# Hash attention and adapter routing: single transposes between score matmuls, value matmuls by key block, crossbar turns, a last pair by thirds

## The chip, the cores and the metric

The kernel runs on one core of a Trainium2 chip. The metric is the time of one execution on the device, in microseconds (us), lower is better. A profiled execution gives the trace: start and duration of every instruction on the matmul engine (PE; its weight loads are shown as PEld), on the vector (DVE), scalar (ACT) and GpSimd (POOL) engines, and what the queues (SP's, ACT's and POOL's) issue as DMAs.

## The reference

Two stages. The first is attention in which a query sees only the keys that have the same hash: six sign bits of a random projection.

```python
q_bits = (np.einsum('bhsd,dk->bhsk', q, proj) > 0)     # k_bits likewise
mask = q_bucket[:, :, :, None] == k_bucket[:, :, None, :]
scores = np.where(mask, scale * q @ k.T, -1e9)
attn = np.exp(scores - scores.max(-1)) / (sum + 1e-9)
x = attn @ v                                           # (4, 8, 768, 64)
```

The second takes x as 3072 tokens of 512 features. Each token is routed to the best two of eight adapters of rank 16 and gets their weighted outputs added.

```python
logits = x @ w_gate                       # 512 -> 8
w = softmax over the two largest logits
out = x + sum over the two e of w[e] * (x @ A[e]) @ B[e]
```

There are 4 batches, 8 heads, 768 positions and head size 64. All is float32 outside; the matmuls of scores, values and adapters run in bf16 with float32 sums.

## The kernel before, in words

**Tiling.** Two heads of a batch make a pair; there are 16 pairs, four to a batch, worked off in the loop of `run` (L340). A position sits at partition p, place t (six places), so 768 = 128 x 6. Each pair has 9 slots: a slot computes 1024 columns of scores (keys on partitions, queries along the row) into one of two PSUM tiles `s` (L178), and ACT takes their exp into `P` in SBUF (L193). Twelve key blocks of 768 columns fill the nine slots.

**The hash mask is part of the score matmul.** Operand `aug` holds 71 rows: 64 of q or k, 6 sign rows of plus or minus one half, and one constant row. The sign products take away so much where a bit differs that the exp vanishes. A uniform tiny weight (the matrix `eps`, L70) is added in the value sum, so that a query with no key in its bucket averages all values.

**What prepares a pair.** `load` (L107) issues q, k and v of a pair on SP's queue, two pairs ahead. `trans` (L135) turns q and k on PE, four 128x128 blocks at a time into a PSUM tile `t`, and DVE copies them to `qkT` (L147). `hash` (L149) multiplies by the projection in four 128x32 tiles of PE; DVE makes signs, and SP issues eight small DMAs that carry them to the sign rows of `aug` (L164). `cast` (L168) brings q and k to bf16 in `aug`, both halves on DVE (L172).

**What follows the scores.** `pvmm` (L196) sums P times V per query block: six key blocks and the uniform one, seven matmuls of 65 columns (64 values and the sum of weights). `norm` (L212) divides. `xtrans` (L231) turns x for the adapter matmuls on PE, `lgz` (L243) computes logits and the rank-16 products, `route` (L254) picks two adapters and weights the products, `zmtrans` (L284) turns these, and `delta` (L296) multiplies by B, adds x and stores.

**Order.** Every engine's order is the order of the calls, written out by hand in `run`. The adapter stage of a finished batch lies in two later pairs (`moe_slot`, L312): logits and routing in one, six deltas in the next. After the last pair the adapter stage of the last batch stands alone (L369 to L381).

```python
                if s == 0:
                    self.load(p + 2)
                    self.norm(p - 1, 0)
                    self.trans(p + 1, 1)
```

PSUM: two `s` tiles of two banks, two `t` tiles, one for value sums, one (`m`) for the adapter stage. [...]

Of the kernel before, what the change touches and what calls it, by code (L numbers as in the profile page):

```python
# [19 lines left out]
class Emitter:  # L20


    def __init__(self, ctx, tc, q, k, v, proj, w_gate, A, Bm, out):
# [11 lines left out]
        self.n_pairs = B * H // 2  # L35
# [6 lines left out]
        one = lambda n: ctx.enter_context(tc.tile_pool(name=n, bufs=1))  # L42
        self.singles = one("singles")
        self.natp = ctx.enter_context(tc.tile_pool(name="natp", bufs=3))
        self.qktp = ctx.enter_context(tc.tile_pool(name="qktp", bufs=2))
        self.sgp = ctx.enter_context(tc.tile_pool(name="sgp", bufs=2))
        self.pp = ctx.enter_context(tc.tile_pool(name="pp", bufs=2))
        self.xp = ctx.enter_context(tc.tile_pool(name="xp", bufs=2))
        self.smallp = ctx.enter_context(tc.tile_pool(name="smallp", bufs=4))
        ps = lambda n, b: ctx.enter_context(  # L50
            tc.tile_pool(name=n, bufs=b, space=bass.MemoryType.PSUM))
        self.ps_s = ps("ps_s", 2)
        self.ps_t = ps("ps_t", 2)
        self.ps_v = ps("ps_v", 1)
        self.ps_m = ps("ps_m", 1)


        sg = self.singles
        self.ident = sg.tile([P, P], F32, name="ident")
        make_identity(nc, self.ident)  # L60
        self.ident_bf = sg.tile([P, P], BF16, name="ident_bf")
        nc.vector.tensor_copy(out=self.ident_bf, in_=self.ident)

        self.proj2 = sg.tile([P, 32], F32, name="proj2")
        nc.vector.memset(self.proj2, 0.0)
        nc.sync.dma_start(out=self.proj2[0:64, 0:6], in_=proj)
        nc.sync.dma_start(out=self.proj2[64:128, 6:12], in_=proj)

        self.eps = sg.tile([P, P], BF16, name="eps")
        nc.vector.memset(self.eps, 2.0 ** -56)  # L70

        self.aug = []
        for i in range(2):
            a = sg.tile([P, 4, S], BF16, name=f"aug{i}")
            for h in range(2):
                nc.vector.memset(a[64:96, 2 * h, :], 1.0)
                nc.vector.memset(a[64:96, 2 * h + 1, :], -1.5)
            self.aug.append(a)

        self.vb = []  # L80
        for i in range(3):
            a = sg.tile([P, 2, T + 1, D + 1], BF16, name=f"vb{i}")
            nc.gpsimd.memset(a[:, :, 0:T, D:D + 1], 1.0)
            nc.gpsimd.memset(a[:, :, T:T + 1, D:D + 1], float(T))
            self.vb.append(a)
        nD = self.Dm // P
        self.nD = nD
        self.wa = sg.tile([P, nD, self.LZ], BF16, name="wa")
        self.Bcat = sg.tile([self.ER, self.Dm], BF16, name="Bcat")
        self.w_gate, self.A, self.Bm = w_gate, A, Bm  # L90

        self.nat, self.vn, self.qkT, self.sgn, self.P_, self.pv = {}, {}, {}, {}, {}, {}
        self.x, self.xb, self.xT, self.lz, self.tp = {}, {}, {}, {}, {}
        self.rt, self.zm, self.zmT, self.acc, self.sc = {}, {}, {}, {}, {}

    def load_moe(self):
        nc, P = self.nc, self.P
        nc.gpsimd.dma_start(out=self.wa[:, :, 0:self.E],
                            in_=self.w_gate.rearrange("(t p) e -> p t e", p=P))
        for t in range(self.nD):  # L100
            nc.gpsimd.dma_start(
                out=self.wa[:, t, self.E:].rearrange("p (e r) -> p e r", e=self.E),
                in_=self.A[:, t * P:(t + 1) * P, :].rearrange("e p r -> p e r"))
        nc.gpsimd.dma_start(out=self.Bcat, in_=self.Bm.rearrange("e r d -> (e r) d"))


    def load(self, p):  # L107
        if p >= self.n_pairs:
            return
        nc = self.nc  # L110
        b, h = p // self.PPB, 2 * (p % self.PPB)
        n = self.natp.tile([self.P, 2, 2, self.T * self.D], F32, tag="nat", name=f"nat{p}")
        for i, src in enumerate((self.q, self.k)):
            nc.sync.dma_start(out=n[:, i], in_=src[b, h:h + 2].rearrange(
                "h (p t) d -> p h (t d)", t=self.T))
        vn = self.natp.tile([self.P, 2, self.T, self.D], F32, tag="vn", name=f"vn{p}")
        nc.sync.dma_start(out=vn.rearrange("p h t d -> p h (t d)"), in_=self.v[b, h:h + 2].rearrange(
            "h (p t) d -> p h (t d)", t=self.T))
        self.nat[p], self.vn[p] = n, vn

    def vcast(self, p):
        if p >= self.n_pairs:
            return
# [9 lines left out]


    def trans(self, p, g):  # L135
        if p >= self.n_pairs:
            return
        nc, P, D = self.nc, self.P, self.D
        if g == 0:
            self.qkT[p] = self.qktp.tile([P, 2 * self.S], F32, tag="qkT", name=f"qkT{p}")  # L140
        ps = self.ps_t.tile([P, 512], F32, tag="t", name=f"tr{p}_{g}")
        for j in range(4):
            idx, u = divmod(4 * g + j, 3)
            nc.tensor.transpose(out=ps[:, j * P:(j + 1) * P],  # L144
                                in_=self.nat[p][:, idx % 2, idx // 2, u * P:(u + 1) * P],
                                identity=self.ident)
        nc.vector.tensor_copy(out=self.qkT[p][:, g * 512:(g + 1) * 512], in_=ps)  # L147

    def hash(self, p):  # L149
        if p >= self.n_pairs:  # L150
            return
        nc = self.nc
        ps = self.ps_t.tile([self.P, 384], F32, tag="t", name=f"hs{p}")
        for j in range(4):
            nc.tensor.matmul(out=ps[32 * j:32 * j + 32, :], lhsT=self.proj2,  # L155
                             rhs=self.qkT[p][:, j * 384:(j + 1) * 384], start=True, stop=True)
        sgn = self.sgp.tile([self.P, 384], BF16, tag="sgn", name=f"sgn{p}")
        nc.vector.tensor_scalar(out=sgn, in0=ps, scalar1=0.0, scalar2=0.5,  # L158
                                op0=ALU.is_gt, op1=ALU.subtract)
        aug = self.aug[p % 2]  # L160
        for j in range(4):
            av = aug[64:70, j, :].rearrange("p (u e c) -> p u e c", e=2, c=self.P)
            for e in range(2):
                nc.sync.dma_start(out=av[:, :, e, :],  # L164
                                  in_=sgn[32 * j + 6 * e:32 * j + 6 * e + 6, :].rearrange(
                                      "p (u c) -> p u c", c=self.P))

    def cast(self, p, e):  # L168
        if p >= self.n_pairs:
            return  # L170
        av = self.aug[p % 2][0:64].rearrange("p j (u e c) -> p (j u) e c", e=2, c=self.P)
        self.nc.vector.tensor_scalar(  # L172
            out=av[:, :, e, :],
            in0=self.qkT[p][64 * e:64 * e + 64, :].rearrange("p (j c) -> p j c", c=self.P),
            scalar1=2.0 ** -5, scalar2=None, op0=ALU.mult)


    def score(self, p, s):  # L178
        nc, S, P = self.nc, self.S, self.P
        if s == 0:  # L180
            self.P_[p] = self.pp.tile([P, 2 * self.T * S], BF16, tag="P", name=f"P{p}")
        aug = self.aug[p % 2]
        ps = self.ps_s.tile([P, 1024], F32, tag="s", name=f"s{p}_{s}")
        at, end = s * 1024, (s + 1) * 1024
        while at < end:
            kt, q0 = divmod(at, S)
            h, kt = divmod(kt, self.T)
            n = min(512 - at % 512, S - q0)
            o = at - s * 1024
            nc.tensor.matmul(out=ps[:, o:o + n], lhsT=aug[0:71, 2 * h + 1, kt * P:(kt + 1) * P],  # L190
                             rhs=aug[0:71, 2 * h, q0:q0 + n], start=True, stop=True)
            at += n
        nc.scalar.activation(out=self.P_[p][:, s * 1024:end], in_=ps, func=ACT.Exp, scale=128.0)  # L193


    def pvmm(self, p, h, i0, i1):  # L196
        if p < 0:
            return
        nc, S, T, D = self.nc, self.S, self.T, self.D
        vb = self.vb[p % 3]  # L200
        if i0 == 0:
            self.pv[p, h] = self.ps_v.tile([self.P, T, D + 1], F32, tag="v", name=f"pv{p}_{h}")
        pv = self.pv[p, h]
        base = h * T * S
        for i in range(i0, i1):
            for kt in range(T + 1):
                o = base + kt * S + i * self.P
                lhsT = self.P_[p][:, o:o + self.P] if kt < T else self.eps
                nc.tensor.matmul(out=pv[:, i, :], lhsT=lhsT, rhs=vb[:, h, kt, :],  # L209
# [220 lines left out]
```

The softmax here doesn't subtract the row's maximum and nothing guards it: scores larger than these inputs give would overflow.

## Time and profile before

| | |
|---|---|
| three timed executions | 214.92, 220.12, 220.92 us; median 220.12 |
| the profiled execution, first to last instruction | 216.4 us |
| busy: PE, DVE, ACT, POOL | 178.0, 142.9, 144.1, 63.4 us |
| score exps (L193) | 144, mean 1024 ns |
| value matmuls (L209), with P and with eps | 1152 and 192 |
| float32 transposes of q and k (L144) | 192 |
| hash matmul passes (L155) | 128 |
| q and k casts on DVE (L172) | 32, mean 998 ns |
| sign DMAs (L164) | 128 of 4.5 KB, 720 ns to issue (median) |
| loads of q, k, v | 48 of 384 KB |
| DMA traffic | 26.39 MB, mean 122 GB/s |

Busy time of an engine is the time in which at least one of its instructions ran. Matmuls are pipelined: one's duration is longer than the distance to the next. Idle time is put down to what ended it, the releaser.

### The profile page before, as it was taken

How to read it: one execution, taken by the hardware profiler on the slowest of the kernel's cores; microseconds unless marked ns; L12 is line 12 of the kernel's file. 1: busy time of each engine (PE TensorE's matmuls, PEld its weight loads, DVE VectorE, ACT ScalarE, POOL GpSimd, SP SyncE). 2: the span in 40 equal slices, each digit the busy share in tenths (PEclk: the TensorE clock that was granted, in tenths of full speed). 3: DMA queues.
4: the chain of work that ended last, by engine and by line, in shares of the span. 5: the costliest groups of instructions: out<-in, count | busy, mean ns of one | idle time of the engine just before them, and what ended most of it. 6: DMA issues, size and time to landing. Idle time of an engine off the chain costs nothing.

```text
span 216.4 us, 5569 instructions
## 1 busy us (share of the span) xinstructions
PE 178.0 (82%) x2288; PEld 123.5 (57%) x2288; DVE 142.9 (66%) x303; ACT 144.1 (67%) x153; POOL 63.4 (29%) x98
## 2 busy tenths in 40 slices
PE   1647999999999997998979987989999879774341
PEld 0314286865868674756656866657678656463200
DVE  7771528675686768698756689796766875634541
ACT  2003679998999987677969976868999858730000
POOL 1694420623416050604133503305144110101000
PEclk9995569999999999999999999999999999997555
DMA  5895406062442616180746042533815000420024
GB/s 144 293 25 82 169 11 217 9 224 71 160 156 76 224 22 209 9 309 11 253 168 215 15 152 76 191 132 141 283 46 186 3 9 3 197 100 0 0 118 173
DMA packets 22874, 26.39 MB, mean 122 GB/s; under 512 B 8897, under 2 KB 21313, under 8 KB 22849
## 3 DMA queue, kind: packets, MB, share of 16 engines
q1 hardware_dynamic: 18016, 25.77, 35.2%
q0 software_dynamic: 4832, 0.27, 3.9%
q8 instruction: 18, 0.29, 0.6%
q14 instruction: 8, 0.06, 0.1%
HBM read 19.42 MB, written 6.29 MB: 119 GB/s over the span
## 4 chain that ended last, share of the span: by engine, by line
PE 52%; DVE 22%; DMA 9%; SPq 8%; issue 5%; ACT 2%; POOLq 0%; POOL 0%; DVEq 0%
PE s L190 20%; PE pv L209 12%; SPq L164 7%; PE tr L144 7%; PE hs L155 5%; DVE acc L303 5%; DMA nat<-in_k_dram 5%; PE dl L301 3%; DMA aug<-sgn 3%; DVE aug L172 3%; DVE sgn L158 2%; PE xtp L238 2%; DVE zm L276 2%; DMA nat<-in_q_dram 2%; DVE x L225 2%
## 5 line engine op out<-in xcount | busy, mean ns | idle before, releaser
L193 ACT ACTIVATE P<-s 128x1024 bf16<-128x1024 f32 x144 | 141.6, 1024 | 47.1 <-PE s L190 43.6
L190 PE MATMUL s<-aug 71*128 71x512 bf16 (+1 forms) x384 | 89.9, 336 | 5.0 <-DMA aug<-sgn 4.8
L209 PEld LDWEIGHTS <-P 128*128 128x128 bf16 x1152 | 51.3, 98 | 14.8 <-DVE x L225 1.0
L209 PE MATMUL pv<-vb,P 128*128 128x65 bf16 x1152 | 53.8, 194 | 0.9 <-DVE x L225 0.9
L190 PEld LDWEIGHTS <-aug 71*128 71x128 bf16 x384 | 32.5, 100 | 28.8 <-issue 13.0
L229 POOL CAST xb<-x 128x768 bf16<-128x768 f32 x16 | 13.2, 825 | 115.3 <-DVE x L225 115.3
L147 DVE COPY qkT<-tr 128x512 f32<-128x512 f32 x48 | 33.0, 690 | 14.1 <-PE tr L144 12.5
L144 PE MATMUL tr<-ident,nat 128*128 128x128 f32 x192 | 32.9, 296 | 8.1 <-DMA nat<-in_q_dram 3.9
L209 PE MATMUL pv<-vb,eps 128*128 128x65 bf16 x192 | 37.4, 195 | 0.0
L144 PEld LDWEIGHTS tr<-ident,nat 128*128 128x128 f32 x192 | 25.2, 152 | 14.4 <-issue 5.6
L172 DVE TENSOR_SCALAR aug<-qkT 64x1536 bf16<-64x1536 f32 x32 | 31.9, 998 | 0.9
L223 DVE RECIPROCAL ri<-pv 128x6 f32<-128x6 f32 x32 | 6.2, 193 | 29.5 <-PE pv L209 29.4
L303 DVE SCALAR_TENSOR_TENSOR acc<-dl,rt,x 128x512 f32<-128x512 f32 x24 | 17.9, 745 | 6.0 <-PE dl L301 6.0
L209 PEld LDWEIGHTS <-eps 128*128 128x128 bf16 x192 | 18.9, 98 | 0.0
L225 DVE TENSOR_TENSOR x<-pv,ri 128x384 f32<-128x384 f32 x32 | 17.8, 557 | 1.2
L126 POOL CAST vb<-vn 128x768 bf16<-128x768 f32 x16 | 13.3, 833 | 13.7 <-DMA vn<-in_v_dram 13.7
L128 POOL TENSOR_TENSOR vs<-vn 128x384 f32<-128x384 f32 x16 | 16.7, 1044 | 0.0
L301 PE MATMUL dl<-Bcat,zmT 128*128 128x512 bf16 x24 | 10.3, 431 | 7.7 <-DVE acc L303 6.8
L155 PE MATMUL hs<-qkT,proj 128*32 128x384 f32 x128 | 15.8, 542 | 0.0
L158 DVE TENSOR_SCALAR sgn<-hs 128x384 bf16<-128x384 f32 x16 | 8.9, 558 | 8.6 <-PE hs L155 7.0
L250 PE MATMUL lz<-wa,xT 128*128 128x136 bf16 x96 | 7.7, 235 | 4.3 <-DVE zm L276 3.6
L238 PE MATMUL xtp<-ident_bf,xb 128*128 128x128 bf16 x96 | 8.0, 219 | 3.0 <-POOL xb L229 1.4
(35 smaller groups left out, 79.6 us busy)
## 6 DMA issues: line engine op xcount, KB each, us to landing
nat<-in_q_dram SPq DMA_DIRECT2D x16, 384.0 KB
nat<-in_k_dram SPq DMA_DIRECT2D x16, 384.0 KB
vn<-in_v_dram SPq DMA_DIRECT2D x16, 384.0 KB
out_dram<-acc SPq DMA_DIRECT2D x12, 512.0 KB
aug<-sgn SPq DMA_DIRECT2D x128, 4.5 KB
wa<-in_moe_A_dram POOLq DMA_DIRECT2D x4, 32.0 KB, 3.1
Bcat<-in_moe_B_dram POOLq DMA_DIRECT2D x1, 128.0 KB, 3.5
proj<-in_proj_dram SPq DMA_DIRECT2D x2, 1.5 KB
```

Of the source, the lines that this page charges most:

```text
L128: nc.gpsimd.tensor_add(out=s3, in0=vn[:, :, 0:3, :], in1=vn[:, :, 3:6, :])
L144: nc.tensor.transpose(out=ps[:, j * P:(j + 1) * P], in_=self.nat[p][:, idx % 2, idx // 2, u * P:(u + 1) * P], identity=self.ident)
L147: nc.vector.tensor_copy(out=self.qkT[p][:, g * 512:(g + 1) * 512], in_=ps)
L155: nc.tensor.matmul(out=ps[32 * j:32 * j + 32, :], lhsT=self.proj2, rhs=self.qkT[p][:, j * 384:(j + 1) * 384], start=True, stop=True)
L164: nc.sync.dma_start(out=av[:, :, e, :], in_=sgn[32 * j + 6 * e:32 * j + 6 * e + 6, :].rearrange("p (u c) -> p u c", c=self.P))
L172: self.nc.vector.tensor_scalar(out=av[:, :, e, :], in0=self.qkT[p][64 * e:64 * e + 64, :].rearrange("p (j c) -> p j c", c=self.P), scalar1 ...
L190: nc.tensor.matmul(out=ps[:, o:o + n], lhsT=aug[0:71, 2 * h + 1, kt * P:(kt + 1) * P], rhs=aug[0:71, 2 * h, q0:q0 + n], start=True, stop=True)
L193: nc.scalar.activation(out=self.P_[p][:, s * 1024:end], in_=ps, func=ACT.Exp, scale=128.0)
L209: nc.tensor.matmul(out=pv[:, i, :], lhsT=lhsT, rhs=vb[:, h, kt, :], start=(kt == 0), stop=(kt == T))
L225: nc.vector.tensor_tensor(out=self.x[b][:, :, c:c + D], in0=pv[:, :, 0:D], in1=ri.unsqueeze(2).to_broadcast([P, T, D]), op=ALU.mult)
L301: nc.tensor.matmul(out=ps, lhsT=self.zmT[b][:, i * P:(i + 1) * P], rhs=self.Bcat, start=True, stop=True)
L303: nc.vector.scalar_tensor_tensor(out=self.acc[b][:, i, :], in0=ps, scalar=self.rt[b][:, i:i + 1], in1=self.x[b][:, i, :], op0=ALU.mult, op ...
```

## The change

The class keeps its stages but nearly every function and the whole order are new.

- **Transposes and copies.** `T1` transposes one 128x128 block; `score` takes a list of such calls and puts one after each of its matmuls. Each of the four operands (q and k of two heads) has its own PSUM tile and a copy of 384 columns (`tcopy`). `aug` is laid out by halves (places 0 to 2, then 3 to 5), so that key block kt is place `tok(kt)`.
- **Cast.** One half on DVE, the other on POOL.
- **Hash.** The two partition halves are multiplied separately, in 64x32 tiles of PE, into two PSUM tiles; four sign DMAs of six rows of 1536 bytes instead of eight.
- **Values.** `uni` adds the uniform weight for all six query blocks in one matmul of 390 columns; `pvk` then runs by key block, all six query blocks for one key block, so a key block can start when its own exps are there.
- **Turn.** `turn` casts x to bf16 on POOL and issues a transposing DMA on SP's queue in place of six PE transposes and a DVE copy. The second last pair keeps PE's way (`to_bf`, `turn_pe`), the last has its own.
- **Order.** Loads are three pairs ahead and split over slots 5, 6 and 7; the adapter stage is spread over four pairs (`moe1`); the adapter's weights are loaded in pairs 2 and 3. PSUM is now two `s`, one `m`, one `n`, two `v`.
- **Start.** Loads by heads on two queues, twelve matmuls on zeros, and for pair 0 and half of pair 1 hash matmuls that write their result at the sign rows' partitions, so that DVE puts signs into `aug` itself.
- **Last pair.** Scores run by thirds of the queries (two places of six at a time); values, norm, turn, logits and routing follow each third.

```diff
-        for j in range(4):
-            idx, u = divmod(4 * g + j, 3)
-            nc.tensor.transpose(out=ps[:, j * P:(j + 1) * P],
-                                in_=self.nat[p][:, idx % 2, idx // 2, u * P:(u + 1) * P],
-                                identity=self.ident)
-        nc.vector.tensor_copy(out=self.qkT[p][:, g * 512:(g + 1) * 512], in_=ps)
+    def T1(self, p, j, u, n=False):
...
+        nc.tensor.transpose(out=self.tr[p, j][:, u * P:(u + 1) * P],
+                            in_=self.nat[p][:, j % 2, j // 2, u * P:(u + 1) * P],
+                            identity=self.ident)
+    def tcopy(self, p, j, eng=None):
...
+        f = self.nc.scalar.copy if eng == "act" else self.nc.vector.tensor_copy
+        f(out=self.qkT[p][:, j, :], in_=self.tr[p, j][:, 0:384])
+    def cast(self, p, e, js=slice(0, 4), eng=None, psum=False):
...
+            (nc.gpsimd if eng == "pool" else nc.vector).tensor_scalar(
+                out=out, in0=in_, scalar1=2.0 ** -5, scalar2=None, op0=ALU.mult)
+    def hash(self, p, js=(0, 1, 2, 3)):
...
+        for j in js:
+            for e in range(2):
+                nc.tensor.matmul(out=ps[e][32 * j:32 * j + 32, 0:384],
+                                 lhsT=self.proj3[64 * e:64 * e + 64, :],
+                                 rhs=self.qkT[p][64 * e:64 * e + 64, j, :], start=True, stop=True)
+    def sign(self, p, js=(0, 1, 2, 3)):
...
+        for e in range(2):
+            nc.vector.tensor_scalar(out=sgn[r, e, :], in0=ps[e][r, 0:384], scalar1=0.0, scalar2=0.5,
+                                    op0=ALU.is_gt, op1=ALU.subtract)
...
+        for j in js:
+            nc.sync.dma_start(out=aug[64:70, j, :],
+                              in_=sgn[32 * j:32 * j + 6, :, :].rearrange("b e c -> b (e c)"))
+    def score(self, p, s, between=()):
...
+            nc.tensor.matmul(out=out, lhsT=aug[0:71, 2 * h + 1, kt * P:(kt + 1) * P],
+                             rhs=rhs, start=True, stop=True)
+            at += w
+            if between:
+                f = between.pop(0)
+                if f:
+                    f()
+        nc.scalar.activation(out=self.P_[p][:, s * 1024:end], in_=ps, func=ACT.Exp, scale=128.0)
...
+    def uni(self, p, h):
...
+        self.nc.tensor.matmul(out=pv, lhsT=self.eps,
+                              rhs=self.vb[p % 3][:, h, T:T + 1, :].to_broadcast([self.P, T, D + 1]),
+                              start=True, stop=False, skip_group_check=True)
+    def pvk(self, p, h, *kts):
...
+        for kt in kts:
+            for i in range(T):
+                o = (h * T + kt) * S + i * P
+                self.nc.tensor.matmul(out=pv[:, i, :], lhsT=self.P_[p][:, o:o + P],
+                                      rhs=vb[:, h, self.tok(kt), :], start=False,
+                                      stop=(kt == T - 1), skip_group_check=True)
+    def turn(self, p):
...
+        nc.gpsimd.tensor_copy(out=xb, in_=self.x[b][:, :, hp * P:(hp + 1) * P])
+        nc.sync.dma_start_transpose(out=self.xT[b][:, hp, :, :], in_=xb.rearrange("p t f -> p (t f)"))
+    def start(self):
...
+        for i in range(12):
+            nc.tensor.matmul(out=w, lhsT=self.wz[:, 0:128], rhs=self.wz, start=True, stop=True)
...
+        for j in (0, 1):
+            for f in self.tb(0, j, j == 1):
+                f()
+        self.tcopy(0, 0)
+        self.hash_here(0, 0, [h0[:, 0], h0[:, 1]])
+        self.tcopy(0, 1, "act")
+        self.hash_here(0, 1, [h1[:, 0], h1[:, 1]])
...
+        self.sign_here(0, 0, 0, h0[:, 0])
+        self.sign_here(0, 0, 1, h0[:, 1])
+        self.sign_here(0, 1, 0, h1[:, 0])
...
+    def slot(self, p, s):
...
+        t = TS.get(p, {0: (p + 1, 1, 0), 1: (p + 1, 3, 1), 5: (p + 2, 0, 0), 7: (p + 2, 2, 0)}).get(s)
+        self.score(p, s, self.tb(*t) if t else ())
+        if s == 3 and p != 1:
+            self.norm(p - 1, 1)
+            (self.to_bf if last else self.turn)(p - 1)
...
+        self.moe1(p, s)
+        if s == 8 and not last and p:
+            self.norm(p, 0)
+        if t:
+            self.tcopy(*t[:2])
+        if p > 1:
+            if s == 2:
+                self.cast(p + 1, 0)
+                self.cast(p + 1, 1, eng="pool")
+            if s == 3:
+                self.hash(p + 1)
+                self.sign(p + 1)
...
+        PV = {0: [(-1, 1, 2)], 1: [(-1, 1, 3)], 2: [(-1, 1, 4), (-1, 1, 5)], 4: [(0, 0, -1), (0, 0, 0), (0, 0, 1)],
+              5: [(0, 0, 2)], 6: [(0, 0, 3), (0, 0, 4)], 7: [(0, 0, 5)], 8: [(0, 1, -1), (0, 1, 0), (0, 1, 1)]}
...
+        if s == 5:
+            self.loadqk(p + 3, 0)
+        if s == 6:
+            self.loadqk(p + 3, 1)
+            self.vcast(p + 1)
+        if s == 7:
+            self.loadv(p + 2)
+    def end(self):
...
+        self.pv3(2, 2)
...
+        self.norm3(2, "act")
+        self.delta(b, 0, S)
+        self.turn3(2)
+        for i in J:
+            self.lgz(b, J, i, (3,))
+        self.route1(b, J)
+        self.route_exp(b, J)
+        self.route2(b, I)
+        self.zt(b, (I,), m)
+        self.route2(b, J)
+        self.zt(b, (J,))
+        self.delta(b, 3, S)
+        self.store(b, 0)
...
```

In the tables of `slot`, a value entry (d, h, k) means key block k of head h of pair p+d, and k = -1 the uniform one. `moe1` places the rest in pairs p of the next batch: logits of three places in slots 5 to 7 of its second and third pair, with routing in slots 7 and 8; their turn in slot 5 of its third and fourth pair; deltas in slots 6 and 8 of the fourth pair and 4, 6, 7 and 8 of the pair after that.

## The prediction

> **What bounds the kernel now.** I read the busy time by stage first. The columns are stretch, length, busy us of PE, PEld, DVE, ACT and POOL with instruction counts, granted clock, DMA share and GB/s.
>
> ```profile
> 0.00:18.83 18.83, 7.87 (x29) 3.81 (x30) 12.28 (x18) 1.28 (x1) 12.16 (x26) 0.94 0.85 141
> 18.83:191.76 172.93, 161.03 (x2171) 114.59 (x2169) 119.95 (x252) 142.34 (x150) 50.38 (x71) 0.97 0.38 128
> 191.76:216.40 24.64, 9.13 (x90) 5.13 (x90) 10.71 (x34) 0.45 (x2) 0.83 (x1) 0.62 0.16 65
> ```
>
> The first score exp starts at 18.83 and the last ends at 191.76. So there is a head of 18.8 us, a stream of 172.9 and a tail of 24.6. In the stream PE is busy 93%, ACT 82%. The waits agree: ACT waits for scores, PE hardly waits for anything.
>
> ```profile
> ACT P L193 <- PE s L190: 43.6, 52, 16.8
> ```
>
> Next come single pairs, in the same columns: the first, a plain one, and one that carries the adapter stage of a finished batch.
>
> ```profile
> 18.83:31.90 13.07, 12.81 (x87) 7.48 (x86) 5.07 (x8) 8.92 (x9) 3.41 (x4) 0.56 0.28 95
> ...
> 59.80:69.00 9.20, 9.20 (x136) 6.74 (x135) 6.48 (x11) 8.61 (x10) 3.46 (x6) 1.00 0.40 135
> ...
> 78.60:91.60 13.00, 11.31 (x166) 8.59 (x165) 9.92 (x35) 9.31 (x11) 3.90 (x6) 1.00 0.30 97
> ```
>
> A plain pair is PE from end to end. The first runs at a clock of 0.56. An adapter pair loses 3.8 us; five of the sixteen (13.0, 12.1, 12.9, 12.4, 13.0) do. A matmul's own duration includes its latency, so its price on PE is the distance between starts in the timeline (start, us):
>
> ```profile
> 159.17 0.60 PE L190 MATMUL s<-aug 71*128 71x512 bf16 x2
> 159.60 0.60 PE L144 MATMUL tr<-ident,nat 128*128 128x128 f32 x4
> 160.07 0.59 PE L190 MATMUL s<-aug 71*128 71x256 bf16 x3
> ...
> 160.69 0.20 PE L209 MATMUL pv<-vb,eps 128*128 128x65 bf16 x1
> 160.72 0.35 PE L209 MATMUL pv<-vb,P 128*128 128x65 bf16 x6
> 160.92 0.19 PE L209 MATMUL pv<-vb,eps 128*128 128x65 bf16 x1
> ...
> 161.50 0.85 PE L155 MATMUL hs<-qkT,proj 128*32 128x384 f32 x8
> 162.29 0.61 PE L190 MATMUL s<-aug 71*128 71x512 bf16 x2
> ```
>
> 512 columns: 0.43/2 = 0.215 us; 256 columns: about half; a transpose 0.11; a value matmul 0.032; the hash 0.79; six bf16 transposes of x 0.34 (starts at 164.94 and 165.28). A plain pair: 12x0.215+12x0.11 (3.9) + 84x0.032 (2.7) + 12x0.11 (1.3) + 0.8 + 0.34 = 9.0, and about 0.2 around the hash.
>
> [...] The trace agrees for the four 128x32 tiles: 8 passes in 0.79 us, where one alone lasts 0.5. [...] beside each other both of these lengthen, against usual values of 0.95 and 1.0.
>
> ```profile
> 25.16 1.25 DVE L172 TENSOR_SCALAR aug<-qkT 64x1536 bf16<-64x1536 f32 x1
> ...
> 25.55 1.71 POOL L128 TENSOR_TENSOR vs<-vn 128x384 f32<-128x384 f32 x1
> ```
>
> [...] 768 elements cast in 0.83 us, 384 added in 1.04. [...]
>
> **The change part by part.**
> *Head.* The first q and k loads are halved and go out on two queues; 12 matmuls on zeros precede the first transposes; signs of pair 0 go straight into aug, without a DMA. The matmuls start near 1.2 and cost 0.215 to 0.43 each, so they end between 3.8 and 6.3; I take 5.5, when the first halves are down too (the whole q was at 3.9). Then 6 transposes (0.11 to 0.28 each in the cold head), a 384-column copy of about 0.55 (0.69 for 512), two hash steps of about 0.4: 7.6. Three signs in DVE's order at 0.5 each: 9.2; a score: first exp at **9.9** (8.7 to 12). Two issues on ACT's queue hide in its idle head. Pair 0 at full clock: 10 us, not 13.
>
> *PE per pair.* Removed: 12 eps matmuls (0.38), six transposes of x (0.34), part of the gap round the hash. Added: two uniform matmuls of 390 columns (0.33). Hash: 16 passes for 8; 0.8 if the row halves run together, 1.6 if not; I take 0.8[...]. Single transposes keep 0.11; between two 256-column scores their 0.14 us weight load may show. So 8.7. The adapter work is now spread: per batch 24 logit matmuls at 0.072 (0.87 for 12 in the tail), six transposes and six deltas, about 3.3, or 0.8 a pair: 9.5. Successive transposes mostly use different PSUM tiles, m and n; those in slots 5 and 7 share m with a slot between, in which DVE empties it. PE alone asks for **9.3 to 9.7**.
>
> *DVE.* Four copies at 0.55, one cast (0.95), two signs (0.56), two norms (0.76), and the adapter's 8.9 a batch spread over four: 2.2+0.95+1.1+1.5+2.2 = 8.0; it fits. The copy of xT (0.55) is gone.
>
> *POOL.* Value casts 2.8, xb 0.83, and a new cast of 64x1536: 1.67 at the rate of the 0.83 cast, 4.2 at the two-input rate; I take 1.67. The six weight loads (0.9 each) move to pairs 2 and 3, where POOL has room.
>
> *SP.* In each pair the turn is issued ahead of the four sign DMAs, and waits for xb. Behind it queue signs, then q, k and v loads, which are three pairs ahead and have a whole pair of slack. So the signs are what is late. From the first score of a pair: last transposes 2.0, copy 2.55, DVE cast 3.5, then the POOL cast [...]5.2, xb 6.0. The turn's issue costs at least the 0.45 us of a plain load; I take 0.8 and 1.7 as the top, a guess of two or three such issues. Two signs (the first head needs two) at 0.45 to 0.72 each, now with longer rows; take 0.5. Landing took 2.35 us after the issue before:
>
> ```profile
> 47.33 3.07 DMA aug<-sgn
> ```
>
> (0.72 of it is the issue.) Sum 6.0+0.8+1.0+2.3 = **10.1** us after the pair's first score, between 9.6 and 11.6. Next pair's first score cannot start earlier, so this, just above PE's own 9.5, is the period I take. In the pairs after a routing step DVE starts about 1 us late, which can add.
>
> *Tail.* Value sums and norm now come by thirds, so after the last exp only one third is left. DVE's list behind it: norm 0.5, acc 0.75, copies 0.6, routing of two groups 0.66+1.1+1.1, five acc at 0.745: 8.4; value matmuls before it 0.4, round trips to PE and ACT about 1.2. Then the last store, 3.6 (216.4 less the end of the last acc at 212.76). Tail **13.6** (12 to 15), not 24.6.
>
> *Sum.* Head 9.9; pair 0 10; pair 1, with its own schedule, 9.7; 13 pairs at 10.1 = 131.3; last pair, few transposes and no hash, 9.3; tail 13.6: 183.8. The profiled execution spans 216.4, the median of the three runs is 3.7 above it, so **187.5**.
>
> **The rivals.** With P the period, the time is 56.2 + 13P.
> (A) As summed, P 9.7 to 10.8: 182 to 197. Chance 0.55.
> (B) The turn and its signs bound the stream outright, P 10.8 to 12.2 (POOL's cast slower, or a turn of 2 us): 197 to 215, middle 206. For it: SP's chain is serial[...]. Against: 0.45 us is what a load of twice the size costs to issue. 0.20.
> (C) The chain hides and PE alone sets P, 9.2 to 9.7: 176 to 182; up to 3 less with a short head and tail. For it: ACT's exps need only 9x0.92 = 8.3 (four in a row take 3.77, one 1.02). 0.17.
> (D) Slower: issuing one turn holds SP for over 3.7 us, 2.9 more than taken; then P is 13.0 and the time 225. At 5 us it is 242. It decides from there since everything later stands behind it on SP. No transposing DMA is in this trace to exclude it. 0.06.
> That the change does nothing would need PE's gain and the shorter ends all lost; 0.02 for between. A measurement here tells apart about 2%.
>
> **How the numbers follow.** Likeliest 187.5. The range leaves out the fast half of C and most of D, and takes in the larger part of B: 174 to 206. Faster by over 2% (under 215.7): A, C and nearly all of B, 0.90; within 2%: 0.04; slower: 0.06.
>
> **What would show it.** First exp near 10; plain pairs and adapter pairs alike near 10; PE waiting for the sign DMA at the first score of a pair, a few tenths each, with the turn ahead of it on SP; hash runs of about 0.8; tail near 13.6. Wrong would be: a turn row on SP of several us, a POOL cast far over 1.7, hash runs of 1.6, or a stream in which DVE's copies keep PE waiting for m and n.

## The result: slower, and the profile after

The changed kernel takes **239.24 us** (237.56 to 240.93, four runs), the kernel before beside it 220.28 (214.92 to 220.92): 1.106 times as long, 95% interval 1.086 to 1.125. The forecast was 187.5, with 206 at the top of its range. The profiled execution spans 239.1. Executions over 1.5% above the fastest of the same kernel are left out of comparisons as slow: three of the four of experiment 1, none of the changed kernel.

Busy time by stage of the changed kernel, cut at its first and last score exp, in the columns used before (length, then PE, PEld, DVE, ACT and POOL, clock, DMA share, GB/s):

```profile
0.00:10.04 10.04, 8.30 (x37) 3.65 (x39) 5.86 (x12) 3.38 (x6) 6.43 (x20) 1.00 0.75 255
10.04:223.42 213.38, 184.23 (x2119) 124.89 (x2118) 116.86 (x281) 143.38 (x151) 135.23 (x105) 0.86 0.43 117
223.42:239.10 15.68, 5.85 (x47) 2.56 (x46) 9.15 (x34) 0.84 (x4) 0.40 (x1) 0.73 0.26 100
```

Head and tail came down, by 8.8 and 9.0 us. The stream lost it all and more: 213.4 us for 172.9. POOL's busy time in it went from 50 to 135 us, and PE's clock from 0.97 to 0.86. The waits (us in total, times, longest) name what PE lacks:

```profile
ACT P L252 <- PE s L245: 69.3, 75, 4.8
...
PE s L245 <- DMA aug<-sgn: 24.1, 12, 3.8
```

The kernel before had few of these waits. Its score matmuls, as one group (busy us, mean ns of one, idle before and what ended most of it):

```profile
L190 PE MATMUL s<-aug 71*128 71x512 bf16 (+1 forms) x384 | 89.9, 336 | 5.0 <-DMA aug<-sgn 4.8
```

That is 4.8 us in all. Now PE waits 12 times, 2 us on average, for the signs that the first score of a pair needs. The chain of waits (start, us, what) says why the signs are late. This is one pair of it, from the last copy of q and k to the next pair's first score:

```profile
50.63 0.57 DVE qkT L167
51.20 0.02 issue
51.23 0.02 POOLq L178
51.24 0.11 issue
51.36 4.78 POOL aug L178
56.13 0.06 issue
56.19 0.83 POOL xb L304
57.02 0.02 issue
57.04 1.24 SPq L305
58.28 0.05 issue
58.33 0.02 SPq L205
58.35 0.04 issue
58.38 0.72 SPq L205
59.10 0.05 issue
59.16 2.36 DMA aug<-sgn
61.51 0.05 issue
61.56 0.39 PE s L245
```

POOL's cast of 4.78 us stands first, then xb, the bf16 copy of x that only the turn needs; then the turn on SP; then the signs behind it on the same queue. The groups by shape (busy us, mean ns of one, idle before) price the cast:

```profile
L178 POOL TENSOR_SCALAR aug<-qkT 64x1536 bf16<-64x1536 f32 x13 | 61.9, 4761 | 57.7 <-DVE qkT L167 57.6
...
L178 POOL TENSOR_SCALAR aug<-qkT 64x768 bf16<-64x768 f32 x6 | 12.8, 2125 | 2.0 <-DVE qkT L167 1.8
...
L304 POOL CAST xb<-x 128x768 bf16<-128x768 f32 x14 | 11.5, 822 | 2.5 <-DVE x L295 1.7
```

Both 768-element rows turn float32 into bf16 on POOL. The one that also multiplies by 2^-5 takes 2.6 times as long.

The timeline of the next pair (start, us, engine) shows that the data was not late, only its DMA:

```profile
64.22 4.76 POOL L178 TENSOR_SCALAR aug<-qkT 64x1536 bf16<-64x1536 f32 x1 [2.92 <-DVE qkT L167]
...
65.97 1.02 DVE L201 TENSOR_SCALAR sgn<-hs 128x384 bf16<-128x384 f32 x2 [0.24 <-PE hs L189]
...
69.05 0.82 POOL L304 CAST xb<-x 128x768 bf16<-128x768 f32 x1
...
69.90 1.25 SPq L305 DMA_TRANSPOSE xT<-xb  x1
...
71.25 2.91 SPq L205 DMA_DIRECT2D aug<-sgn  x4
...
73.92 0.61 PE L245 MATMUL s<-aug 71*128 71x512 bf16 x1 [3.10 <-DMA aug<-sgn]
```

The signs are ready at 66.99 and go out from 71.25: 4.3 us of standing behind a transfer that nothing near needs. PE waits 3.1 us, and after it the clock is half (stages again):

```profile
73.90:79.00 5.10, 5.08 (x37) 3.83 (x38) 2.07 (x3) 2.41 (x3) 0.83 (x1) 0.50 0.70 235
```

### The profile page after: what moved, and what is told of

Read it like the earlier page. It is cut to its first block, busy times and chain, and to the rows that moved or that the text cites. A ratio compares the mean times of both kernels' runs of the same rounds, so it can differ in the third digit from the quotient of the medians.

```text
span 239.1 us, 5410 instructions
## 1 busy us (share of the span) xinstructions
PE 198.4 (83%) x2200; PEld 131.1 (55%) x2200; DVE 131.9 (55%) x325; ACT 147.6 (62%) x160; POOL 142.1 (59%) x126
## 4 chain that ended last, share of the span: by engine, by line
PE 57%; POOL 10%; DVE 10%; DMA 9%; issue 5%; SPq 5%; ACT 1%; DVEq 0%; POOLq 0%; ACTq 0%
PE s L245 23%; PE pv L275 10%; DMA aug<-sgn 9%; PE tr L159 9%; POOL aug L178 7%; PE hs L189 4%; SPq L205 2%; SPq L305 2%; PE lz L380 2%; PE warm L486 2%; PE dl L450 2%; DVE sgn L201 2%; DVE acc L454 2%; POOL xb L304 1%; DVE qkT L167 1%
## 5 line engine op out<-in xcount | busy, mean ns | idle before, releaser
L245 PE MATMUL s<-aug 71*128 71x256 bf16 (+1 forms) x396 | 112.7, 361 | 24.6 <-DMA aug<-sgn 24.1
L178 POOL TENSOR_SCALAR aug<-qkT 64x1536 bf16<-64x1536 f32 (+2 forms) x21 | 77.0, 3665 | 62.2 <-DVE qkT L167 59.4
L167 DVE COPY qkT<-tr 128x384 f32<-128x384 f32 x62 | 34.3, 555 | 53.0 <-PE tr L159 52.8
L159 PE MATMUL tr<-ident,nat 128*128 128x128 f32 x192 | 50.5, 306 | 0.3 <-DVE sgn L201 0.3
L201 DVE TENSOR_SCALAR sgn<-hs 128x384 bf16<-128x384 f32 (+1 forms) x32 | 16.4, 552 | 11.2 <-PE hs L189 11.1
L189 PE MATMUL hs<-qkT,proj 64*32 64x384 f32 x232 | 16.7, 591 | 0.0
L178 DVE TENSOR_SCALAR aug<-qkT 64x1536 bf16<-64x1536 f32 (+1 forms) x17 | 15.4, 905 | 0.5
L450 PE MATMUL dl<-Bcat,zT 128*128 128x512 bf16 x24 | 10.3, 448 | 1.9 <-DVE acc L454 1.0
L263 PE MATMUL pv<-vb,eps 128*128 128x390 bf16 x30 | 10.7, 358 | 0.0
L380 PEld LDWEIGHTS <-xT 128*128 128x128 bf16 x96 | 7.1, 97 | 2.7 <-issue 1.1
```

Source lines behind the costliest of these rows:

```text
L159: nc.tensor.transpose(out=self.tr[p, j][:, u * P:(u + 1) * P], in_=self.nat[p][:, j % 2, j // 2, u * P:(u + 1) * P], identity=self.ident)
L167: f(out=self.qkT[p][:, j, :], in_=self.tr[p, j][:, 0:384])
L178: (nc.gpsimd if eng == "pool" else nc.vector).tensor_scalar(out=out, in0=in_, scalar1=2.0 ** -5, scalar2=None, op0=ALU.mult)
L189: nc.tensor.matmul(out=ps[e][32 * j:32 * j + 32, 0:384], lhsT=self.proj3[64 * e:64 * e + 64, :], rhs=self.qkT[p][64 * e:64 * e + 64, j, :] ...
L201: nc.vector.tensor_scalar(out=sgn[r, e, :], in0=ps[e][r, 0:384], scalar1=0.0, scalar2=0.5, op0=ALU.is_gt, op1=ALU.subtract)
L245: nc.tensor.matmul(out=out, lhsT=aug[0:71, 2 * h + 1, kt * P:(kt + 1) * P], rhs=rhs, start=True, stop=True)
```

## The experiments

**Theory 1**: POOL's slow cast holds up xb, xb the turn, and the turn, ahead of the signs on SP, the signs. Cutting this chain at any place brings the period to PE's own, near 10. **Theory 2**: the cold clock drives the loop. **Theory 3**: the new PE order, with single transposes, is slow in itself. For each kernel below I read the mean period from first score to first score and the mean place of each step after the first score, over pairs 3 to 12 (us):

| kernel | time | period | POOL cast | xb ends | turn on SP | second sign issued |
|---|---|---|---|---|---|---|
| changed | 239.24 | 13.56 | 3.49–8.26 | 9.14 | 9.17–10.46 | 12.04 |
| cast on DVE | 202.38 | 10.78 | none | 6.13 | 6.16–7.48 | 9.06 |
| turn after signs | 194.57 | 10.13 | 3.62–8.19 | – | – | 6.92 |
| warm PE | 229.52 | 12.75 | 2.66–7.43 | 8.3 | 8.34–9.65 | 11.23 |
| plain cast on POOL | 200.37 | 10.53 | 2.78–4.96 | 5.9 | 5.87–7.22 | 8.80 |
| plain cast, turn after signs | 192.41 | 9.93 | 2.76–4.94 | 5.83 | 8.54–9.78 | 6.91 |

(The time of the cast on DVE is that of its profiled execution alone, see experiment 1; the other times are medians. With the turn after the signs and POOL's cast slow, xb and turn of some pairs slip into the next one, so a mean has no meaning there.)

**1. The second cast back on DVE**, from pair 2 on.

```diff
-                self.cast(p + 1, 1, eng="pool")
+                self.cast(p + 1, 1)
```

> From pair 2 on, the second half of the q and k cast goes back from POOL to DVE; the turn stays ahead of the signs on SP. If the length of POOL's cast (4.77 us) is what makes the chain late: two casts on DVE end 4.5 us after a pair's first score, norm 5.2, xb 6.1, turn 7.35, two signs and their landing 2.7: period 10.0 instead of 13.4, so 13 x 3.4 = 44 us less, about 195. If the turn holds the signs up by itself, whatever POOL does, the period stays above 12 and the time above 220.

Measured: 202.38 us in one execution (the other three took 205.42 to 207.68), the kernel before beside it 218.24; one execution gives no interval. Some 37 us are gone with one instruction in each of 13 pairs. The period is 10.8, not the 10.0 I gave: PE still waits for the sign DMAs 4 times, 2.9 us in all, and 7.0 us for DVE's sign instruction, which now stands behind two casts in DVE's order.

**2. The turn behind the signs on SP**, everything else as changed, POOL's cast as slow as ever.

```diff
         if s == 3 and p != 1:
             self.norm(p - 1, 1)
-            (self.to_bf if last else self.turn)(p - 1)
+            if last or p < 2:
+                (self.to_bf if last else self.turn)(p - 1)
...
                 self.sign(p + 1)
+                if not last:
+                    self.turn(p - 1)
```

> From pair 2 on, the turn is issued after the four sign DMAs instead of ahead of them; the cast stays on POOL at 4.77 us. If the signs are late only because they stand behind the turn on SP's queue: signs ready 5.7 us after the first score, two issues and landing 2.7: 8.4, hidden; PE sets the period, 9.5 to 10: about 188 to 195. If the slow cast is late by itself (it also writes half of the score operand), or if the sign DMAs are slow beside transposing ones, the period stays above 11 and the time above 205.

Measured: 194.57 us (194.05 to 195.68), 0.896 of before (0.888 to 0.903). One moved call is worth 45 us, more than the gap to the kernel before. The group by shape of this kernel:

```profile
L178 POOL TENSOR_SCALAR aug<-qkT 64x1536 bf16<-64x1536 f32 x13 | 59.8, 4603 | 14.6 <-DVE qkT L167 14.3
```

And its timeline (start, us, engine):

```profile
58.22 1.02 DVE L201 TENSOR_SCALAR sgn<-hs 128x384 bf16<-128x384 f32 x2 [0.23 <-PE hs L189]
...
59.27 2.90 SPq L205 DMA_DIRECT2D aug<-sgn  x4
...
59.84 4.08 POOL L178 TENSOR_SCALAR aug<-qkT 64x1536 bf16<-64x1536 f32 x1
...
63.98 0.82 POOL L304 CAST xb<-x 128x768 bf16<-128x768 f32 x1
...
64.83 1.24 SPq L305 DMA_TRANSPOSE xT<-xb  x1
```

The cast is still 4.6 us on average. But the signs leave 0.03 us after DVE has made them, and cast, xb and turn run beside the scores. No wait of PE for the sign DMAs is left.

**3. Both edits together.**

> Both edits. If the cause is the one chain cast, xb, turn, signs, either cut suffices and this is no better than the better of the two, by less than 2 us, perhaps worse since DVE then carries 9 us of work per pair: 188 to 195. If cast and turn cost separately, it is faster than either by 10 us or more.

Measured: 200.96 us (200.5 to 201.29), 0.925 (0.917 to 0.933): 6.4 us worse than edit 2 alone. With the turn out of the way POOL's cast is covered, and the second cast only loads DVE: PE waits for DVE's sign instruction 7.2 us in all, where it waits 2.4 in edit 2. So 37 and 45 don't add: they are two cuts of one chain.

**4. PE kept warm**: eleven 512-column matmuls on zeros ahead of the first score of pairs 3 to 15; the score overwrites their result.

```diff
+        if s == 0 and p >= 3:
+            for _ in range(11):
+                nc.tensor.matmul(out=ps[:, 0:512], lhsT=self.wz[:, 0:128], rhs=self.wz, start=True, stop=True)
```

> The changed kernel with eleven matmuls on zeros (512 columns, overwritten by the score) ahead of the first score of pairs 3 to 15, where PE waits for the signs: 11 x 0.215 = 2.4 us of work inside a wait of some 3 us. They only keep the clock up. If PE's cold clock after the wait feeds the loop (transposes and hash done 1.7 us later, so cast, turn and signs later): period about 12, time about 220 to 225. If the clock adds nothing to the chain: 239 as before, or up to 13 x 2 more.

Measured: 229.52 us (228.99 to 229.82), 1.055 (1.048 to 1.063): between the two. Its stages show the clock whole across two pairs:

```profile
70.00:96.00 26.00, 24.52 (x300) 16.66 (x301) 13.04 (x39) 17.93 (x21) 17.70 (x14) 1.00 0.40 118
```

DVE's first cast starts 2.53 us into the pair, not 3.36, and the period falls by nearly the same, 0.81. So the cold clock adds 0.8 us a pair by making the transposes that lead the chain slower, some 10 us in all. The other 2.7 us a pair stay. Theory 2 is a part, not the cause.

**5. A plain cast on POOL**: the factor 2^-5, exact in float32, moves into the copies out of PSUM, which DVE does anyway (0.55 us each, with the factor and without). The turn stays ahead.

```diff
-        f = self.nc.scalar.copy if eng == "act" else self.nc.vector.tensor_copy
-        f(out=self.qkT[p][:, j, :], in_=self.tr[p, j][:, 0:384])
...
+            self.nc.vector.tensor_scalar(out=out, in0=in_, scalar1=2.0 ** -5, scalar2=None, op0=ALU.mult)
...
-            (nc.gpsimd if eng == "pool" else nc.vector).tensor_scalar(
-                out=out, in0=in_, scalar1=2.0 ** -5, scalar2=None, op0=ALU.mult)
+            (nc.gpsimd if eng == "pool" else nc.vector).tensor_copy(out=out, in_=in_)
```

> The changed kernel with the scale 2^-5 moved from the casts into the copies out of PSUM, so that POOL's part is a plain cast of 64x1536 instead of a multiplication; order and queues unchanged. If a multiplication on POOL runs at its two-input rate (2.7 ns an element) and a plain cast at 1.08 ns, as xb does: POOL's part 1.7 to 2.4 us instead of 4.77, the turn 2.4 to 3.1 us earlier: period about 10.5 to 11, time about 200 to 205. If the length comes from the shape (64 partitions, three-dimensional) or the neighbour on DVE, it stays at 4 us or more and the time above 230.

Measured: 200.37 us (199.01 to 201.2), 0.913 (0.905 to 0.922). The group by shape:

```profile
L181 POOL CAST aug<-qkT 64x1536 bf16<-64x1536 f32 x13 | 28.3, 2176 | 42.8 <-DVE qkT L170 42.8
```

4.76 has become 2.18, on the same engine, shape and types. This edit alone makes the kernel faster than the one before. PE still waits for the sign DMAs ahead of 7 first scores, 6.0 us in all.

**6. Edit 5 with the turn behind the signs.**

> The plain cast on POOL, and the turn issued after the signs. If only the one chain held the pairs back, PE sets the period as in the run with the late turn alone: 191 to 195, no more than 3 us better. If POOL's cast also delays the score operand in that run, it is 5 us or more better.

Measured: 192.41 us (192.12 to 193.56), 0.879 (0.873 to 0.886). Once the turn is behind, the faster cast is worth only 2 us (194.57 less 192.41), and no wait of PE for the sign DMAs is left. So theory 1 holds, with one correction: each cut breaks the chain, but after a cut at the cast (edits 1 and 5) some of these waits stay, and only the order on the queue takes them all away.

**7. Edit 2 with a slot's transposes in one group after its scores.** The block that issues them between scores goes; the loop after the exp then issues them all.

```diff
-            if between:
-                f = between.pop(0)
-                if f:
-                    f()
```

> The late turn, and the transposes of a slot issued together after its scores instead of one after each score matmul. If single transposes gain nothing by themselves (0.11 us each either way): within 2 us of the run with the late turn alone, 194.6. If they hide their weight loads (0.14 us, twelve a pair): slower by up to 12 x 0.03 x 16 = 6 us; if putting them between scores delays the exps: faster by some us.

Measured: 192.95 us (192.41 to 193.15), 0.881 (0.875 to 0.886): 1.6 us less than edit 2. Single transposes between score matmuls bring nothing here; with the plain cast, grouping takes off 4 us (experiment 9 against 6). Theory 3 fails as the cause: this is 2 to 4 us, and the kernel came out 52 above its forecast.

**8. The turn on PE instead**: xb is cast in slot 3, and six transposes and one DVE copy follow in slot 8; POOL's slow cast stays.

```diff
-            (self.to_bf if last else self.turn)(p - 1)
+            if p:
+                self.to_bf(p - 1)
...
         if s == 8 and not last and p:
+            self.turn_pe(p - 1)
             self.norm(p, 0)
```

> The changed kernel with x turned on PE (six transposes and a DVE copy in slot 8) instead of by the transposing DMA; POOL's cast stays at 4.77 us, nothing stands ahead of the signs on SP. If the wait of SP for the turn is the cause: signs as early as in the run with the late turn, period 10.1 plus 0.34 on PE: 197 to 202. If POOL's cast is late for the score by itself: above 210.

Measured: 210.97 us (207.88 to 210.98), 0.960 (0.951 to 0.969): neither of the two outcomes. SP is free, yet this is 16 us slower than edit 2.

**9. Edit 6 with grouped transposes**, the best of these.

> Plain cast on POOL, turn after the signs, and the transposes of a slot together behind its scores. If the two small gains seen (192.4 with the plain cast, 193.0 with grouped transposes, against 194.6) add up: about 191. If both come from the same slack: 192 to 193.

Measured: **188.45 us** (187.94 to 190.32, five runs), 0.862 (0.857 to 0.867). It beats both kernels. Its stages:

```profile
10.87:172.11 161.24, 154.37 (x2119) 107.30 (x2117) 114.40 (x281) 141.22 (x151) 94.35 (x105) 1.00 0.56 153
```

PE is busy 96% of the stream at full clock: now PE is what bounds it.

**10. Edit 8 with the plain cast**, to see if POOL was what made edit 8 slow.

> Plain cast on POOL, and x turned on PE in slot 8 instead of by the transposing DMA. With the turn on PE and POOL's cast at 4.77 us it was 211.0; if what it lost there against 194.6 was PE waiting for an x that stood behind POOL's cast, that goes now: PE's own 0.34 us a pair and DVE's copy remain, 13 pairs, so 192.4 + 5 to 8 = 197 to 200. If turning on PE costs its time by itself (order on DVE and the shared PSUM tile), it stays near 208.

Measured: 208.36 us (208.19 to 208.57), 0.954 (0.949 to 0.958). POOL's cast was not the reason; the PE turn is. Its timeline at the end of one pair:

```profile
75.13 0.49 PE L320 MATMUL xtp<-ident_bf,xb 128*128 128x128 bf16 x6 [0.66 <-DVE gw L417]
...
76.01 0.53 DVE L321 COPY xT<-xtp 128x768 bf16<-128x768 bf16 x1
...
76.59 0.33 PE L159 MATMUL tr<-ident,nat 128*128 128x128 f32 x1 [0.21 <-DVE xT L321]
...
77.35 3.78 ACT L254 ACTIVATE P<-s 128x1024 bf16<-128x1024 f32 x4 [1.72 <-PE s L247]
```

In PE's order the turn stands behind routing and ahead of the next pair's transposes. PE waits 0.66 us for DVE's routing before the turn and 0.21 for DVE's copy after it, and ACT is left idle 1.72. By the starts on PE in pairs 4 to 12, the six transposes take 0.81 us a pair with the wait ahead of them and the wait behind them 0.2: 1.0 of the 1.05 us by which the period of pairs 3 to 12 exceeds that of edit 6 (10.98 against 9.93). So the turn by a transposing DMA, put behind the signs, saves 16 us against this placement of a PE turn (208.36 less 192.41). Other placements were not tried.

## Why the prediction was wrong, by its own steps

**The step that failed is POOL's cast**: "a new cast of 64x1536: 1.67 at the rate of the 0.83 cast, 4.2 at the two-input rate; I take 1.67". It took 4.77. I priced a multiplication by the row of a plain cast because both have one input tensor. That the two run alike was my estimate: the kernel before had no such multiplication on POOL to show it. With 4.08 us for 1536 elements when DVE's cast is not beside it (2.66 ns each; three casts of edit 2), it runs like the addition of two inputs (1.04 us for 384, 2.7 ns each), and the plain cast of edit 5 in 2.18. The remaining 0.69 us comes beside DVE's cast: casts that start 0.13 us after DVE's 0.95 us cast take 4.77. In the kernel before, an addition on POOL took 1.71 us beside a cast on DVE, against 1.00 otherwise.

**A second error let the first one do its harm**: the top of the range. I had named 4.2 as the other bound and did not carry it through. With it, my own sum gives P = 10.1 + 2.5 = 12.6 and 56.2 + 13 x 12.6 = 220, no change; rival B was stopped at 12.2 and D given 0.06.

Where the time went, against my sum of 183.8 for the profiled execution (239.1):

| term | predicted | measured | us in all |
|---|---|---|---|
| head, to first exp | 9.9 | 10.04 | +0.1 |
| pair 0; pair 1 | 10; 9.7 | 13.3; 11.7 | +5.3 |
| period, 13 pairs | 10.1 | 13.61 | +45.7 |
| last pair | 9.3 | 11.4 | +2.1 |
| tail | 13.6 | 15.7 | +2.1 |

The 3.7 us that I added to come from the profiled execution to the median are 0.1 here (239.24 less 239.1).

The period, step by step (means of pairs 3 to 12, 13.56): POOL's cast ends at 8.26, not 5.2 (+3.06); xb 0.88, not 0.8 (+0.1); the turn 1.32 with its gap, not 0.8 (+0.5); signs and landing together 3.10, not 3.3 (-0.2). That is 10.1 + 3.5. Of the 3.06, longer work is 3.10 and the cold clock 0.8, less 0.85 because POOL's cast starts beside DVE's and not after it.

- **The mechanism held.** The signs behind a turn that waits for xb, which waits for POOL, set the period. That was my chain and rival B's, at a size beyond B's range. Edit 2 shows the queue order to be the decisive link, and edits 1 and 5 the cast.
- **The loop through the clock was left out.** I wrote of "a few tenths" of waiting. After the wait of 3.10 us (73.92) the clock is 0.50 over the next 5 us and the first transposes start 0.43 us apart; after the one of 1.07 (61.56) it is 1.00, and they start 0.22 apart. So the next pair's transposes are later, and so are its signs. Over the first 5 us after the waits of 2.25, 2.70 and 3.75 us the clock is 0.50 too; after four others, of 1.24 to 3.82 us, it is 0.66 to 0.71, after two, of 0.23 and 1.25, it is 1.00. From which length on a wait lowers the clock, these waits do not show. Edit 4 prices it at 0.8 us a pair.
- **Rival D** forecast the outcome, slower, for another reason: a turn that holds SP for over 3.7 us by its own issue. It took 1.25 mostly, 2.51 at most. What held SP was the turn's wait for its input (in the pair above until 69.90, with the signs ready at 66.99).
- **Rival C** and PE's own price were nearly right: freed of the chain, the period is 10.1 (edit 2) or 9.9 (edit 6), against 9.3 to 9.7. The hash ran its 16 passes in 0.81 us at full clock (edits 2 and 6), as taken. The waits for DVE's copies that I listed as a danger did not show in the changed kernel.
- **Pairs 0 and 1** were not worked out; I scaled pair 0 by its clock. The clock was full, but signs made in place come in small steps:

```profile
10.04:23.34 13.30, 12.64 (x97) 5.84 (x97) 8.50 (x17) 9.00 (x9) 12.12 (x12) 1.00 0.38 134
23.34:35.04 11.70, 11.55 (x158) 7.91 (x157) 9.27 (x19) 9.01 (x10) 9.03 (x7) 1.00 0.24 57
```

PE is busy 12.64 of 13.30 us there. By the starts on PE, pair 0 has four groups of four hash passes at 0.77, 1.23, 0.77 and 1.23 us and one of eight at 0.79, 4.8 us in all, where the 16 of a later pair take 0.81. Pair 0 is much the same in every version that I ran (13.2 to 13.3, with grouped transposes 12.2 to 12.5), so it is no part of the loss in the stream. The last pair, 11.4, falls to 9.4 with PE kept warm (edit 4) and to 10.1 in edits 1, 2 and 5; it was not tried apart. Of the tail's 2.1, DVE's work is 0.75 (9.15 busy for 8.4); the rest, round trips and the last store, I did not separate.

## What to carry to other kernels

On SP's queue here a transfer cost its wait for its input as well as its issue, and everything behind it paid: signs that were ready stood 4.3 us. So put a transfer that nobody needs soon behind those that the next stage waits for: that one line was 45 us here. Price an operation on POOL by its own opcode in a trace, and carry the worse bound of an unknown through to the total before giving a range.

## What the runs showed of the hardware

- On POOL, float32 to bf16 with a multiplication by a constant: 1.17, 2.12 and 4.08 to 4.77 us for 64 partitions of 384, 768 and 1536 elements. The plain cast: 0.50, 0.82 and 2.18. The last of these always started near DVE's cast; it was not measured alone.
- A transposing DMA of 128x768 bf16 within SBUF holds SP's queue 1.24 to 1.26 us in most cases and up to 2.51, where a load of 384 KB holds it 0.44 to 0.47 and a sign DMA 0.67 (medians; 0.72 for the sign DMA of the kernel before).
- In the changed kernel the clock was 1.00 over the 5 us after a wait of 1.07 us (61.56), 0.50 after waits of 2.25 and 3.10 (101.13 and 73.92). Over the stream it was 0.86, where it was 1.00 in edit 9. With matmuls on zeros in the wait (edit 4) it was 1.00 across two pairs, and the period 12.75 instead of 13.56.
